# Order of the halves, and how q and k are loaded and transposed, in a sparse-attention and FFN kernel

## The chip, the core and the metric

The kernel runs on one core of a Trainium2 chip. Its engines work in parallel, each on its own queue of instructions in program order: TensorE (PE in the profile, PEld for its weight loads) multiplies and transposes, VectorE (DVE), ScalarE (ACT) and GpSimd (POOL) work element by element, and SyncE (SP) only issues DMAs. ACT and POOL can issue DMAs too. Engines wait for each other on semaphores. SBUF is the working memory with 128 partitions; PSUM holds what TensorE writes. The metric is the device time of one execution in microseconds (us).

## The reference

Four batches, 8 heads, 768 tokens, head dimension 64. Keys are cut into 24 chunks of 32 tokens. For each query an upper bound of its scores in each chunk is made from the chunk's smallest and largest keys; the six best chunks that are not in the future are kept, and softmax attention runs over these alone. The result, as 3072 rows of 512, goes through an FFN with a squared ReLU.

```python
k_min, k_max = min and max of k over each chunk
ub = np.sum(np.maximum(q[:, :, :, None, :] * k_min[:, :, None, :, :],
                       q[:, :, :, None, :] * k_max[:, :, None, :, :]), axis=-1)
ub = np.where(causal, ub, -1000000000.0)
top_chunks = np.argsort(ub, axis=-1)[..., -top_k:]
mask = sel & (pos[:, None] >= pos[None, :])
scores = np.where(mask, scale * q @ k.T, -1000000000.0)
attn = softmax(scores)
x = (attn @ v), heads side by side          # (3072, 512)
h = np.maximum(x @ w_in, 0.0)               # (3072, 2048)
out = h * h @ w_out                         # (3072, 512)
```

## The kernel before

**Tiles and slots.** A half is 384 tokens of one batch (`HB`, three blocks of 128). The work is cut into 32 slots `s`, each one pair of heads `p` of one half, four slots to a half and eight halves, in the order batch 0 first half, batch 0 second half, batch 1 first half, and so on. By causality a first half needs 6 pairs of blocks (query block, key block) a head, a second half 15; these I call light and heavy.

**One slot.** `step_P` gets queries and keys with the head dimension on the partitions, and relu(-q) and relu(q) of the queries. Chunk minima and maxima land in `kbds`. `step_U` multiplies these into the bounds `ub`, takes the sixth largest by MAX8 and writes which chunks fall out (`nsel`). `step_V` transposes that (`qt`) and copies it into the rows of `kqs` beside the queries, where fixed code rows (`codes`) stand beside the keys: a score of an unselected chunk so becomes hugely negative. `step_E` makes scores `ps` and ACT's exponentials `e` (POOL masks the diagonal), `step_F` multiplies with the values `vn` into `po`, and DVE divides into `x` (L386).

**Which way keys and queries are transposed.** The first two halves (`ON_PE = 2`) are transposed on TensorE, a 128x128 block at a time (`step_T`, L204): three for k and three for q in each slot. From PSUM, `step_T2` makes the relus on ACT (L212, L213), the chunk extrema on DVE (`extrema`, L181 and L182), and `place` copies keys (DVE) and queries (ACT) into `kqs` (L222). From the third half on, a DMA transpose issued by SP (`tr`, L250) writes `kqT`, two more DMAs place it in `kqs` (`place_dma`, L234), DVE makes the relus (`relus`, L245 and L246) and folds the chunks of a whole half in steps (`step_K`, L266, parts spread over a slot or two).

**Loads.** POOL issues them and converts fp32 to bf16 in the DMA. A load of k or q (`load_n`, L85) brings 128 tokens of all heads, so each contiguous run is one token of one head, 64 elements. Values come four heads at a time over all 768 tokens (`load_v`, L101). `w_in` and `w_out` come in two loads each. The first two pairs of the first half are loaded as fp32 by SP and ACT and cast on chip.

**The order of the work is written out by hand.** `later` maps a slot to what is issued at two points of it (`go`): loads, DMA transposes, code DMAs. The FFN of a half starts when its attention ends (`step_X` transposes `x`, on TensorE for the first, second and last half, by DMA otherwise); its pieces, 16 up products (L431, ReLU on ACT at L438, for half of the first half's on DVE at L436, square on DVE at L440) and 12 down pieces (L450), stand in `queue` and are taken by `f1` between the steps of later slots, by a `quota` for each slot. The up products share two PSUM buffers (`psF`), the down products one (`psY`), the rest of attention two (`psA`) and the scores three (`psS`).

Of the kernel before, what the change touches and what calls it, by code (L numbers as in the profile page):

```python
# [14 lines left out]
CH = 32  # L15
# [13 lines left out]
ON_PE = 2  # L29
# [5 lines left out]
def kernel(  # L35
# [40 lines left out]
    kn0 = epool.tile([128, HT, NP, 2 * D], BF16, tag="kn0", name="kn0")  # L76
# [6 lines left out]
    def load_n(n, b, j):  # L83
        t = nat[n, b, j] = work.tile([128, DM], BF16, tag=f"{n}n", bufs=7, name=f"{n}n")
        nc.gpsimd.dma_start(  # L85
            out=t.rearrange("p (h d) -> p h d", d=D),
            in_=(q if n == "q" else k)[b, :, 128 * j:128 * (j + 1)]
            .rearrange("h p d -> p h d"))

    def load_k0(j):  # L90
        nc.gpsimd.dma_start(
            out=kn0[:, j, 2:NP, :].rearrange("p a (h d) -> p (a h) d", h=2),
            in_=k[0, 4:H, 128 * j:128 * (j + 1)].rearrange("h p d -> p h d"))
# [10 lines left out]


    staged = {}
    for p, n in ((0, "k"), (0, "q"), (1, "k"), (1, "q")):
        x = epool.tile([128, HT, 2, D], F32, tag=f"st{n}{p}", name="stage")
        for hh in range(2):
            (nc.sync if n == "k" or p else nc.scalar).dma_start(  # L110
                out=x[:, :, hh, :],
                in_=(k if n == "k" else q)[0, 2 * p + hh, 0:HB]
                .rearrange("(j p) d -> p j d", p=128))
        staged[n, p] = x
# [6 lines left out]
    make_identity(nc, ident)  # L121
    for j in range(HT):
        load_k0(j)
        for h in range(2):
            load_q0(j, h)
    load_v(0, 0, 4)
# [46 lines left out]
    slots = [(b, half, p) for b in range(B) for half in range(2) for p in range(NP)]  # L173
# [3 lines left out]
    def extrema(kt, s):  # L177
        b, half, p = slots[s]
        km = work.tile([128, 2, 12], BF16, tag="km", name="km")
        kv = kt.rearrange("p (c j) -> p c j", j=CH)  # L180
        nc.vector.tensor_reduce(km[:, 0, :], kv, axis=AX.X, op=ALU.min)  # L181
        nc.vector.tensor_reduce(km[:, 1, :], kv, axis=AX.X, op=ALU.max)  # L182
# [3 lines left out]

    def step_cast(p):
        nc.vector.tensor_copy(kn0[:, :, p, :].rearrange("p j (h d) -> p j h d", h=2),
                              staged["k", p])
        nc.scalar.copy(qn0[:, :, p, 1:3, :], staged["q", p])  # L190

    def step_T(s, kp, qp):

        b, half, p = slots[s]
        t = st.setdefault(s, {})
        for n, (pool, tag) in enumerate((kp, qp)):
            x = t["kq"[n]] = pool.tile([128, HB], BF16, tag=tag, name="t" + "kq"[n])
            for j in range(HT):
                if s < NP:
                    src = (qn0[:, j, p, 1:3, :].rearrange("p h d -> p (h d)") if n  # L200
                           else kn0[:, j, p, :])
                else:
                    src = nat["kq"[n], b, HT * half + j][:, 128 * p:128 * (p + 1)]
                nc.tensor.matmul(x[:, 128 * j:128 * (j + 1)], lhsT=src, rhs=ident,  # L204
                                 is_transpose=True, start=True, stop=True)

    def step_T2(s):
# [4 lines left out]
        nc.scalar.activation(qr[:, 0, c:], t["q"][:, c:], ACT.Relu, scale=-1.0)  # L212
        nc.scalar.activation(qr[:, 1, c:], t["q"][:, c:], ACT.Relu)  # L213
# [5 lines left out]
    def place(s, n, copy):  # L219
        b, half, p = slots[s]  # L220
        for h in range(2):
            copy(kqs[b % 2][QROW[h]:QROW[h] + D, h, p, 2 * half + "kq".index(n), :],  # L222
                 st[s][n][D * h:D * h + D])
# [8 lines left out]
    def place_dma(hb):  # L232
        for h in range(2):
            nc.sync.dma_start(  # L234
                out=kqs[hb // 2 % 2][QROW[h]:QROW[h] + D, h, :,
                                     2 * (hb % 2):2 * (hb % 2) + 2, :],
                in_=half_T(hb)[D * h:D * h + D])

    def relus(s):
        hb, p = s // NP, s % NP  # L240
        qT = tT[hb][:, p, 1, :]
        c = 128 * (1 - hb % 2)
# [5 lines left out]
    def tr(hb, n, j):  # L248
        b, half = hb // 2, hb % 2
        nc.sync.dma_start_transpose(  # L250
            out=half_T(hb)[:, :, "kq".index(n), 128 * j:128 * (j + 1)],
            in_=nat.pop((n, b, HT * half + j)))

    def step_K(hb):

        b, half = hb // 2, hb % 2
# [24 lines left out]
    def step_P(s):  # L281
# [3 lines left out]
        step_T(s, *((F, Y) if s < NP + 2 else (Y, A)))  # L285
# [109 lines left out]
    def step_X(hb, pe):  # L395
# [21 lines left out]
        for c in ("u" * NFI) if hb == 0 else "ddudu" "duuduud" "uuduuduu" "uuuu":  # L417
# [10 lines left out]
    def ffn_up(hb, xT, f):  # L428
# [6 lines left out]
        if hb == 0 and f % 2:  # L435
            nc.vector.tensor_scalar_max(ht, ph[:, 0:HB], 0.0)  # L436
        else:
            nc.scalar.activation(ht, ph[:, 0:HB], ACT.Relu)  # L438
# [4 lines left out]
    def ffn_down(hb, py, t, c, act, tail):  # L443
# [9 lines left out]
        if c == 3:  # L453
# [5 lines left out]
            r0 = HB * hb + 128 * t  # L459
# [22 lines left out]
    def load_half(hb):  # L482
        b, half = hb // 2, hb % 2
        return [(load_n, n, b, HT * half + j) for n in "kq" for j in range(HT)]

    for i, x in enumerate(load_half(1)):
        at(i // 3 - 1, *x)
    at(1, load_v, 0, 4, 8)
    for g in range(2):
        at(1, load_w_in, 1024 * g, 1024 * g + 1024)  # L490
    for i, x in enumerate(load_half(2)):
        at(2 + i // 3, *x)
    at(0, codes, 0, 1, nc.sync.dma_start)
    at(1, clear)
    for half in range(2):
        at(2, codes, 1, half, nc.sync.dma_start)
# [159 lines left out]
```

## Time and profile before

| | us |
|---|---|
| median of three runs | 306.0 (303.69 to 306.05) |
| profiled execution, its own time | 306.22 |
| span of that execution in the profile | 304.5 |
| TensorE busy | 257.7 |
| ScalarE busy | 172.4 |
| VectorE busy | 168.4 |
| GpSimd busy | 92.6 |

The mean granted clock of TensorE was 0.966 of full speed. A row of the profile names line, engine and operation, the tile written and the tiles read, then how many, the busy time, the mean in ns, and the idle time of the engine before them with what ended it. Matmul ends are modelled, so the pace of a run of matmuls is read from start to start.

### The profile page before, as it was taken

The numbers are of one execution on the slowest core, as the hardware profiler recorded it, in microseconds if no ns is written. First come the engines' busy times: TensorE is split into PE (matmuls) and PEld (weight loads), VectorE is DVE, ScalarE is ACT, GpSimd is POOL, SyncE is SP. The second block draws the span as 40 slices with busy tenths as digits, with TensorE's granted clock in tenths as the row PEclk, the third lists the DMA queues.
The fourth block names the chain that finished last, engine by engine and source line by source line (L and its number), as shares of the span: only waits on it lengthen the run. The fifth ranks groups of instructions, "written<-read, shape, count | busy, mean of one in ns | idle before, by whom it ended". The sixth has DMA issues, their size and how long they took to land.

```text
span 304.5 us, 6200 instructions
## 1 busy us (share of the span) xinstructions
PE 257.7 (85%) x2232; PEld 156.6 (51%) x2260; DVE 168.4 (55%) x657; ACT 172.4 (57%) x370; POOL 92.6 (30%) x133
## 2 busy tenths in 40 slices
PE   1576798398939969998969979998979999999994
PEld 1355465155515636665526636665546566655541
DVE  6668597583266625854276626753497445433421
ACT  4559398245606646784536648783547667843410
POOL 8868322123932133443331223530112101100000
PEclk9997799899969999999989999999999999999999
DMA  9999999969999095899989198694661310101001
GB/s 159 174 132 174 196 166 196 156 102 109 119 156 139 35 153 102 96 175 120 141 131 128 22 155 108 115 171 68 133 138 38 86 37 0 37 31 40 34 36 69
DMA packets 114062, 33.30 MB, mean 109 GB/s; under 512 B 103280, under 2 KB 109936, under 8 KB 114032
## 3 DMA queue, kind: packets, MB, share of 16 engines
q0 software_dynamic: 74736, 13.24, 60.5%
q1 hardware_dynamic: 38496, 19.47, 31.4%
q8 instruction: 17, 0.28, 0.4%
q10 hardware_dynamic: 800, 0.20, 0.3%
q14 instruction: 13, 0.11, 0.1%
HBM read 27.26 MB, written 6.29 MB: 110 GB/s over the span
## 4 chain that ended last, share of the span: by engine, by line
PE 55%; DMA 21%; DVE 10%; issue 4%; ACT 3%; SPq 3%; POOL 2%; POOLq 0%; ACTq 0%
PE py L450 20%; PE ph L431 20%; DMA kqT<-kn 8%; PE ps L351 8%; DMA kn<-in_k_dram 6%; PE po L376 5%; DMA vn<-in_v_dram 4%; DMA xT<-x 3%; DVE km L266 3%; DVE h L440 2%; ACT e L356 2%; DVE x L386 1%; SPq L413 1%; SPq L250 1%; POOL qn L96 1%
## 5 line engine op out<-in xcount | busy, mean ns | idle before, releaser
L356 ACT ACTIVATE e<-ps 128x512 bf16<-128x512 f32 x192 | 96.8, 549 | 51.6 <-PE ps L351 51.5
L431 PE MATMUL ph<-xT,w_in 128*128 128x384 bf16 x512 | 104.7, 333 | 9.6 <-DVE ht L436 5.1
L450 PE MATMUL py<-w_out,h 128*128 128x512 bf16 x356 | 92.6, 383 | 3.6 <-ACT ob L456 2.1
L360 POOL TENSOR_SCALAR_AFFINE_SELECT e<-e 128x384 bf16<-128x384 bf16 x64 | 34.0, 532 | 168.2 <-ACT e L356 165.9
L438 ACT ACTIVATE ht<-ph 128x384 bf16<-128x384 f32 x120 | 59.5, 502 | 44.4 <-PE ph L431 43.9
L440 DVE TENSOR_TENSOR h<-ht 128x384 bf16<-128x384 bf16 x128 | 47.9, 375 | 61.3 <-ACT ht L438 60.7
L431 PEld LDWEIGHTS <-w_in 128*128 128x128 bf16 x512 | 47.7, 99 | 40.1 <-issue 14.5
L351 PE MATMUL ps<-kq 128*128 128x384 bf16 (+2 forms) x320 | 59.7, 291 | 3.4 <-DVE kq L327 2.1
L450 PEld LDWEIGHTS <-h 128*128 128x128 bf16 x384 | 35.6, 98 | 34.8 <-issue 3.7
L351 PEld LDWEIGHTS <-kq 128*128 128x128 bf16 x320 | 28.4, 102 | 23.9 <-issue 4.6
L376 PEld LDWEIGHTS <-e 128*128 128x128 bf16 x672 | 26.5, 100 | 6.2 <-issue 1.6
L376 PE MATMUL po<-vn,e 128*128 128x65 bf16 x672 | 27.8, 196 | 1.1 <-DMA vn<-in_v_dram 0.8
L305 DVE MAX8 m<-ub 128x8 f32<-128x24 f32 (+1 forms) x160 | 16.6, 171 | 11.7 <-PE ub L298 11.6
L85 POOL DMA_DIRECT2D kn<-in_k_dram x21 | 18.9, 906 | 0.3 <-issue 0.2
L85 POOL DMA_DIRECT2D qn<-in_q_dram x21 | 18.6, 892 | 0.1
L333 PE MATMUL qt<-ident,nsel 128*128 128x128 bf16 x72 | 9.0, 226 | 11.3 <-DVE nsel L306 11.2
L386 DVE TENSOR_TENSOR x<-po,r 128x384 bf16<-128x384 f32 x32 | 17.8, 558 | 1.1
L266 DVE TENSOR_TENSOR km<-kqT 128x768 bf16<-128x768 bf16 x12 | 6.7, 558 | 18.2 <-DMA kqT<-kn 11.8
L456 ACT COPY ob<-py 128x512 f32<-128x512 f32 x19 | 11.1, 585 | 9.6 <-PE py L450 9.5
L337 DVE COPY kq<-qt 64x384 bf16<-64x384 bf16 (+1 forms) x28 | 8.8, 315 | 13.1 <-PE qt L333 13.1
L333 PEld LDWEIGHTS <-nsel 128*128 128x128 bf16 x72 | 5.4, 99 | 18.2 <-DVE nsel L306 15.6
L266 DVE TENSOR_TENSOR km<-km 128x384 bf16<-128x384 bf16 (+3 forms) x48 | 13.2, 274 | 0.8
(59 smaller groups left out, 163.9 us busy)
## 6 DMA issues: line engine op xcount, KB each, us to landing
out_dram<-ob SPq DMA_DIRECT2D x24, 256.0 KB, 2.2
kq<-kqT SPq DMA_DIRECT2D x12, 384.0 KB, 5.5
vn<-in_v_dram POOLq DMA_DIRECT2D x8, 384.0 KB, 9.0
kn<-in_k_dram POOLq DMA_DIRECT2D x21, 128.0 KB, 5.0
qn<-in_q_dram POOLq DMA_DIRECT2D x21, 128.0 KB, 7.3
w_in<-in_moe_w_in_dram POOLq DMA_DIRECT2D x2, 1024.0 KB, 12.6
w_out<-in_moe_w_out_dram POOLq DMA_DIRECT2D x2, 1024.0 KB, 17.6
kq<-oneh SPq DMA_DIRECT2D x6, 192.0 KB, 7.4
```

Source lines behind the costliest of these rows:

```text
L85: nc.gpsimd.dma_start(out=t.rearrange("p (h d) -> p h d", d=D), in_=(q if n == "q" else k)[b, :, 128 * j:128 * (j + 1)] .rearrange("h p d ...
L266: nc.vector.tensor_tensor(y, x[:, :, :, 0:m], x[:, :, :, m:2 * m], op=op)
L305: nc.vector.max(out=m8[:, j, hh, :], in_=ub[:, j - j0, hh, :])
L351: nc.tensor.matmul(ps[:, at:at + 128 * m], lhsT=kqs[b % 2][:, hh, p, 2 * (j // HT), 128 * (j % HT):128 * (j % HT + 1)], rhs=qc(s, hh)[:, c ...
L356: nc.scalar.activation(e[:, 512 * n + lo:512 * n + hi], ps[:, lo:hi], ACT.Exp, scale=float(scale))
L360: nc.gpsimd.affine_select(out=d, in_=d, compare_op=ALU.is_ge, fill=0.0, base=0, channel_multiplier=-1, pattern=[[0, 3], [1, 128]])
L376: nc.tensor.matmul(po[:, hh, i, :], lhsT=t["e"][hh][:, c:c + 128], rhs=vn[b % 2][:, 2 * p + hh, j, :], start=(j == 0), stop=(j == iq))
L386: nc.vector.tensor_mul(x[:, :, 128 * p:128 * (p + 1)].rearrange("p j (h d) -> p h j d", h=2), po[:, :, :, 0:D], r.to_broadcast([128, 2, HT ...
L431: nc.tensor.matmul(ph[:, 0:HB], lhsT=w_in[:, ki, 128 * f:128 * (f + 1)], rhs=xT[:, ki, :], start=(ki == 0), stop=(ki == NKI - 1))
L438: nc.scalar.activation(ht, ph[:, 0:HB], ACT.Relu)
L440: nc.vector.tensor_mul(h, ht, ht)
L450: nc.tensor.matmul(py[t], lhsT=h2[hb, f][:, 128 * t:128 * (t + 1)], rhs=w_out[:, f, :], start=(f == 0), stop=(f == NFI - 1))
```

## The change

Four things change together. The halves come in the order (batch 0 first, batch 1 first, batch 0 second, batch 1 second), then batches two and three as before (`ORDER`); the second half in time is now a light one and the third a heavy one. Three halves instead of two are transposed on TensorE (`ON_PE = 3`). For these, except the queries of the first, a load puts 4 consecutive tokens of a head on one of 96 partitions (`load_packed`), and a head's 64 columns are transposed 96 tokens at a time (16 transposes a slot instead of 6). The transposed tokens so lie in four strides of 96, and `extrema`, the relus and `place` read them from PSUM in token order. The issue times of nearly all loads, the values' loads (a block of 128 tokens of all heads at a time for the first two batches), the code DMAs, the order of the FFN's pieces and the quotas move with it, and all ReLUs of the FFN go to ACT.

```diff
+ORDER = ((0, 0), (1, 0), (0, 1), (1, 1), (2, 0), (2, 1), (3, 0), (3, 1))
-ON_PE = 2
+ON_PE = 3
+TP = 4
+PP = HB // TP
...
+    def load_packed(n, g, h0=0):
         nc.gpsimd.dma_start(
+            out=packed(n, g)[:, h0:H],
+            in_=rows(n, *ORDER[g], h0, H).rearrange("h (p j) d -> p h (j d)", j=TP))
...
+    def load_vt(b, j):
+        nc.gpsimd.dma_start(
+            out=vn[b % 2][:, :, j, 0:D],
+            in_=v[b, :, 128 * j:128 * (j + 1)].rearrange("h p d -> p h d"))
...
-        kv = kt.rearrange("p (c j) -> p c j", j=CH)
-        nc.vector.tensor_reduce(km[:, 0, :], kv, axis=AX.X, op=ALU.min)
+        kv = kt.rearrange("r (j c e) -> r c j e", j=TP, c=12)
+        nc.vector.tensor_reduce(km[:, 0, :], kv, axis=AX.XY, op=ALU.min)
...
+    def in_order(x):
+        return x.rearrange("r (j p) -> r p j", j=TP)
...
+            for hh in range(2):
+                for j in range(TP):
+                    nc.tensor.matmul(
+                        x[D * hh:D * hh + D, PP * j:PP * j + PP],
+                        lhsT=packed(n, s // NP)[:, 2 * p + hh, D * j:D * j + D],
+                        rhs=ident[0:PP, 0:PP], is_transpose=True, start=True, stop=True)
...
+        for w in range(2):
+            o, i = qr[:, w, c:], t["q"][:, c:]
+            if s >= NP:
+                o, i = by_token(o), in_order(t["q"])[:, c // TP:, :]
+            nc.scalar.activation(o, i, ACT.Relu, scale=(-1.0, 1.0)[w])
...
-            copy(kqs[b % 2][QROW[h]:QROW[h] + D, h, p, 2 * half + "kq".index(n), :],
-                 st[s][n][D * h:D * h + D])
+            copy(by_token(kqs[b % 2][QROW[h]:QROW[h] + D, h, p, 2 * half + "kq".index(n), :]),
+                 in_order(st[s][n][D * h:D * h + D]))
...
-        step_T(s, *((F, Y) if s < NP + 2 else (Y, A)))
+        step_T(s, *((F, Y) if s < NP + 2 else (Y, A) if s < 2 * NP + 1 else (F, A)))
...
-        for c in ("u" * NFI) if hb == 0 else "ddudu" "duuduud" "uuduuduu" "uuuu":
+        for c in ("u" * NFI) if hb == 0 else "dddd" + "uud" * 4 + "u" * 8:
...
-        if hb == 0 and f % 2:
-            nc.vector.tensor_scalar_max(ht, ph[:, 0:HB], 0.0)
-        else:
-            nc.scalar.activation(ht, ph[:, 0:HB], ACT.Relu)
+        nc.scalar.activation(ht, ph[:, 0:HB], ACT.Relu)
...
+    for n in "kq":
+        at(-1, load_packed, n, 1)
     for g in range(2):
-        at(1, load_w_in, 1024 * g, 1024 * g + 1024)
+        at(0, load_w_in, 1024 * g, 1024 * g + 1024)
+    at(0, codes, 1, 0, nc.sync.dma_start)
     at(1, clear)
+    for j in range(HT):
+        at(1, load_vt, 1, j)
+    for n in "kq":
+        at(2, load_packed, n, 2)
+    at(3, codes, 0, 1, nc.sync.dma_start)
     for g in range(2):
-        at(3 + g, load_w_out, 8 * g, 8 * g + 8)
+        at(3, load_w_out, 8 * g, 8 * g + 8)
+    for j in range(HT):
+        at(5, load_vt, 0, HT + j)
+        at(6, load_n, "k", 3, j)
+        at(8, load_n, "q", 3, j)
+        at(9, load_vt, 1, HT + j)
+    at(7, codes, 1, 1, nc.sync.dma_start)
+    for g in range(4, 2 * B):
         for i in range(2 * HT):
+            at(4 * g - 6 + i // HT, load_n, "kq"[i // HT], g, i % HT)
...
-        quota = [(4, 5, 6, 5)[p] if hb == 1 else 9 if p == 0 and hb > 2 else
+        quota = [(4, 4, 4, 6)[p] if hb == 1 else 9 if p == 0 and hb > 2 else
                  7 if p == 3 else 6]
-        if hb < 2 * B - 1 and p == (2 if hb == 1 else 1):
+        if ON_PE - 1 <= hb < 2 * B - 1 and p == (2 if hb < ON_PE else 1):
             parts.extend(step_K(hb + 1))
```

123 lines of the change are left out of this document (55 added, 68 removed).

## The prediction

> **What bounds the kernel now.** I read the page first, then the windows, then the chain of waits, then the timeline around the gaps the chain showed. The page:
>
> ```profile
> span 304.5 us, 6200 instructions
> PE 257.7 (85%) x2232; PEld 156.6 (51%) x2260; DVE 168.4 (55%) x657; ACT 172.4 (57%) x370; POOL 92.6 (30%) x133
> PEclk9997799899969999999989999999999999999999
> DMA  9999999969999095899989198694661310101001
> ```
>
> TensorE (PE) is the bound on average, but not everywhere: the DMA row is full for about the first third, and the lowest clock digits lie in the same third. The windows (start:end, length, then busy us of PE, PEld, DVE, ACT and POOL, the clock, DMA share, GB/s) divide the run into the first half (four slots without FFN work), the second, the third, and all the rest, with three 10 us stretches of them:
>
> ```profile
> 0.00:33.50 33.50, 16.93 (x173) 12.70 (x174) 23.70 (x97) 20.09 (x46) 26.57 (x40) 0.95 1.83 165
> 33.50:73.00 39.50, 31.27 (x317) 20.20 (x320) 27.37 (x96) 23.27 (x48) 10.42 (x14) 0.91 1.38 156
> 73.00:105.40 32.40, 26.59 (x210) 15.28 (x212) 17.88 (x77) 16.19 (x35) 12.90 (x18) 0.89 1.12 113
> 105.40:304.50 199.10, 182.91 (x1539) 108.42 (x1558) 99.42 (x389) 112.89 (x241) 42.67 (x62) 0.99 0.66 90
> ...
> 40.00:50.00 10.00, 9.38 (x107) 6.46 (x105) 9.56 (x30) 9.32 (x21) 1.55 (x3) 1.00 1.41 181
> 50.00:60.00 10.00, 4.86 (x55) 2.82 (x52) 5.17 (x19) 4.39 (x9) 2.44 (x3) 0.92 1.60 169
> 80.00:90.00 10.00, 4.49 (x38) 2.63 (x36) 3.86 (x18) 2.91 (x8) 4.32 (x6) 0.78 2.01 164
> ```
>
> After 105.4 us PE is busy 92% of the time (182.91 of 199.10) and nothing there is edited but load times. What can be won lies before: 50 to 60 and 80 to 90 have PE at half. The chain says what these wait for:
>
> ```profile
> 25.61 12.98 DMA kn<-in_k_dram
> 41.30 15.19 DMA kqT<-kn
> 70.33 5.21 DMA kn<-in_k_dram
> 76.81 5.36 DMA kqT<-kn
> ```
>
> A load of keys, then a DMA transpose of them, once for the third half and once for the fourth. The timeline shows how that reaches PE:
>
> ```profile
> 56.52 0.56 DVE L266 TENSOR_TENSOR km<-kqT 128x768 bf16<-128x768 bf16 x1 [4.63 <-DMA kqT<-kn]
> 58.56 1.44 PE L431 MATMUL ph<-xT,w_in 128*128 128x384 bf16 x4 [4.52 <-DVE ht L436]
> 61.45 1.62 PE L431 MATMUL ph<-xT,w_in 128*128 128x384 bf16 x8
> 85.94 0.56 DVE L266 TENSOR_TENSOR km<-kqT 128x768 bf16<-128x768 bf16 x1 [6.24 <-issue]
> 89.03 0.40 PE L333 MATMUL qt<-ident,nsel 128*128 128x128 bf16 x2 [5.45 <-DVE nsel L306]
> 91.56 1.27 PE L431 MATMUL ph<-xT,w_in 128*128 128x384 bf16 x4
> 93.05 0.81 PE L431 MATMUL ph<-xT,w_in 128*128 128x384 bf16 x4
> ```
>
> The fold of the keys (L266) stands at the head of VectorE's (DVE's) queue and waits for the transposes; FFN and selection work stands behind it, and PE runs dry for 4.52 and 5.45 us. Afterwards the granted clock is at half for a while: four matmuls take 1.44 and 1.27 us against 0.81.
>
> **What goes.** The third half no longer goes through a DMA transpose, so the first wait has no cause left. The fourth half (still by DMA) is loaded from slot 6 and 8 and transposed in slots 8 and 9, two slots ahead of its fold in slot 10, where before the fold of the third came in slot 6 behind loads queued with w_in. And the loads ahead of it shrink:
>
> ```profile
> DMA packets 114062, 33.30 MB, mean 109 GB/s; under 512 B 103280, under 2 KB 109936, under 8 KB 114032
> w_out<-in_moe_w_out_dram POOLq DMA_DIRECT2D x2, 1024.0 KB, 17.6
> ```
>
> Nine packets in ten are under 512 B. A half of k or of q is 3 x 128 tokens x 8 heads = 3072 runs of one token; four tokens to a partition makes 96 x 8 = 768. The k and q of halves two and three and most keys of the first go that way, six DMA transposes and the two placing DMAs of the third vanish, and the values of batch 0's second half move to slot 5. I price these loads at what waits for them, not by bytes.
>
> Stall 1: 4.52 idle, and half speed from 58.56 to about 61.4, which loses half of 2.9, 1.4. Stall 2: 5.45, and half speed from 89.03 to about 92.8, 1.9. Together **-13.3 us**. If a load is late all the same, the fourth half's fold is what waits next (a rival below).
>
> In the first half two transposes waited for loads:
>
> ```profile
> 13.91 0.29 PE L204 MATMUL tk<-ident,kn 128*128 128x128 bf16 x1 [1.36 <-DMA kn<-in_k_dram]
> 15.28 0.29 PE L204 MATMUL tq<-ident,qn 128*128 128x128 bf16 x1 [0.86 <-DMA qn<-in_q_dram]
> ```
>
> One packed load for keys and all of q before v, with four of six code DMAs gone from SP's early queue, should land both before they are needed: 1.36 + 0.86 = 2.2; less a little for the added transposes, **-2.0**.
>
> **What is added on PE.** A pair needs 2 heads x 4 = 8 transposes for k and 8 for q, against 3 and 3, and against none in the third half. First half: +5 x 4 = 20; second: +10 x 4 = 40; third: 16 x 4 = 64; 124 in all. The 20 of the first half and the 20 of slots 4 and 5 (made in slots 2 and 3) fall where PE is busy 16.93 of 33.5 us and cost nothing; without that cover they cost 2.8. The other 84 lie on the path. No 96x64 transpose is in the trace. The nearest are these, three 128x128 transposes in 0.17 us from start to start, 57 ns each, and the weight loads:
>
> ```profile
> 40.16 0.33 PE L204 MATMUL tk<-ident,kn 128*128 128x128 bf16 x3
> 40.33 0.33 PE L204 MATMUL tq<-ident,qn 128*128 128x128 bf16 x3
> 40.50 0.81 PE L431 MATMUL ph<-xT,w_in 128*128 128x384 bf16 x4
> ...
> L204 PE MATMUL tk<-ident,kn 128*128 128x128 bf16 x24 | 3.6, 263 | 7.7 <-DVE kn L188 6.4 <-DMA kn<-in_k_dram 1.4
> ```
>
> By columns it would be 57 x 96/128 = 43 ns; as thinly as the 24 rows ran, 3.6/24 = 150 ns. I take 70, nearer the dense row because these too come in runs of eight: 84 x 70 = **+5.9** (3.6 to 12.6).
>
> The Trainium skill ("TensorE: Matmul & The Clock Gate", section "Weight-path perf modes") says the fast weight load needs a full 128-column weight, and these have 64; by its section "LDWEIGHTS" (columns/1.2) each takes 53 ns to load. Added to 43 ns of matmul unhidden, an estimate of 96 ns, the term would be 8.1; no run so far shows a 64-column load.
>
> **What is added on DVE and ScalarE (ACT).** These rows:
>
> ```profile
> L438 ACT ACTIVATE ht<-ph 128x384 bf16<-128x384 f32 x120 | 59.5, 502 | 44.4 <-PE ph L431 43.9 <-DVE nsel L306 0.4
> L181 DVE TENSOR_REDUCE km<-tk 128x12 bf16<-128x384 bf16 x8 | 4.4, 554 | 1.3 <-PE tk L204 1.2
> L213 ACT ACTIVATE qr<-tq 128x384 bf16<-128x384 bf16 x4 | 2.1, 516 | 0.0
> L222 ACT COPY kq<-tq 64x384 bf16<-64x384 bf16 x8 | 3.8, 473 | 0.1
> L222 DVE COPY kq<-tk 64x384 bf16<-64x384 bf16 x8 | 2.8, 355 | 0.1
> L436 DVE TENSOR_SCALAR ht<-ph 128x384 bf16<-128x384 f32 x8 | 4.4, 555 | 0.7 <-PE ph L431 0.6
> ```
>
> ACT gets two relus (0.516) and two query placements (0.473) in each slot of the third half, 1.98 x 4 = 7.9, and the eight relus of the FFN that DVE did, 8 x 0.502 = 4.0: 11.9 us. It was busy 23.27 + 16.19 of the 71.9 us of halves two and three, so it holds 51.4 of about 64. DVE gets two reductions and two key placements a slot of the third half, 2 x 0.554 + 2 x 0.355 = 1.8, times 4 is 7.3; it loses the 4.4 of L436 and the fold. So no engine is full. But 40 to 50 us shows PE, DVE and ACT over 93% busy at once with PE losing 0.6 us in 10. Bounds: 0 (hidden) to 11.9 (nothing hidden); I take PE's loss in that row over some 25 us of heavy slots, **+1.5**. The order also adds a wait: keys of slots 9 to 11 go into one of the two buffers of the FFN's first product (psF) until DVE has reduced and placed them, about 1.8 us each; on PE the next FFN product, and all behind it, can stand for that buffer. 0 to 5.4; I take half of the 0.50 (L438) in which ACT empties one, 0.25, thrice: **+0.8**.
>
> The strided copy has a row to either side: 355 ns for a copy, 554 ns for a reduction of the same 384 columns. At the second, place costs 0.4 us more a slot on DVE, which has room.
>
> The Trainium skill ("VectorE: DVE Perf Modes", section "Mode 2×_1P") asks step 1 for two 16-bit elements a cycle, which reading every 96th column breaks; it would put the copy at the second row. The 355 against 554 here agrees with such a mode for the unstrided copy.
>
> Orders that cost nothing: heavy and light halves only change places; by the quotas (20+25 pieces of FFN before, 18+25 after) one up and one down product are done later instead of earlier, at the same price on PE. POOL issues 2 DMAs for a half instead of 6, with its masks queued behind fewer. Values in three loads instead of one half-height load are 3072 packets either way. SP loses eight DMAs around the third half. Loads for halves four on are 2 slots ahead of their transposes; PE's 92% there I leave.
>
> **Sum.** -13.3 - 2.0 + 5.9 + 1.5 + 0.8 = -7.1. The profiled execution took 306.2 us for a span of 304.5 and stands 0.2 over the median of 306.0, so **299 us**.
>
> **Rivals.** (a) *More is won.* Transposes at 43 ns (3.6), no engine waits, and a less loaded DMA when the attention output is transposed at 105 us:
>
> ```profile
> 107.98 5.40 DMA xT<-x
> ```
>
> The fourth half's q and the fifth half's k are off the queues by then, and 5.40 could fall to about 3, -2.4: -13.3 - 2.2 + 3.6 - 2.4 = -14.3, 292. Against it: three engines at 93% do not run without waits. (b) *The stall only moves.* w_out (17.6 us to land, its row above) is now issued in slot 3 with the packed loads just ahead, and the fourth half's keys queue behind it; if they come late, the fold in slot 10 holds DVE as at 85.94, and stall 2 (7.4) stays: +0.3, 306. For it: half the chain there is DMA today. Against: four slots lie between load and fold. This is also the case in which packing does nothing, since bytes and not packets set the loads. (c) *Slower: reading PSUM in token order.* Every relu, reduction and placement of halves two and three now reads with a stride of 96. If that runs at half rate, ACT pays 1.98 and DVE 1.8 more a slot; in eight slots, with all three engines near full, the larger is on the path: 15.8, so -7.1 + 15.8 = +8.7, 315. It decides from about 0.9 us a slot, a strided operation 1.45 times as long. For it: no strided read of PSUM is in the trace, and DVE and ACT stood at 9.56 and 9.32 of 10. Against: ACT's time does not differ between 4-byte and 2-byte inputs (502, 516), so it seems to go by elements.
>
> **Numbers.** Forecast (294 to 303) 0.51; more (a, under 294) 0.13; moved stall (b, 303 to 309) 0.16; slower (c, over 309) 0.20. The range 290 to 311 leaves out the best of (a) and most of (c), together just under 0.2, and takes in the transposes' 12.6 (306) and an ACT term of 11.9 (309.5) by themselves. A measurement of this kernel can tell about 1%, 3 us, from no change. Faster: 0.51 + 0.13 = 0.64; within 1%: 0.16; slower: 0.20.
>
> **What would show it.** Right: no wait of DVE for kqT over 1 us before 105 us, the two waits at 13.9 and 15.3 gone, the third half over some 8 us before 105.4; PE busy some 6 to 9 us more in total; 96x64 transposes about 70 ns apart. (a) shows PE over 96% in halves two and three; (b) a wait for kqT or w_out near slot 10; (c) a relu or reduction well over 0.55 us and PE idle behind ACT or DVE. I am wrong if the waits go and the gain does not come: then the added work, not the loads, set these halves.

## The result, and the profile after

The changed kernel takes 294.45 us (median of 4 runs, 292.3 to 296.74), beside 306.02 us (303.69 to 306.85) for the kernel before on the same chip: a ratio of 0.961, 95% interval 0.952 to 0.970. It is 11.6 us faster where 7.1 were forecast. The profiled execution took 295.2 us, 1.8 more than its span. The page of it:

```profile
span 293.4 us, 6470 instructions
PE 260.4 (89%) x2384; PEld 159.8 (54%) x2384; DVE 172.0 (59%) x648; ACT 180.9 (62%) x393; POOL 87.4 (30%) x131
PEclk9999999999999999999999999999999999999999
DMA  8999999908999665999679966997451300010001
DMA packets 98671, 31.74 MB, mean 108 GB/s; under 512 B 84560, under 2 KB 94544, under 8 KB 98640
```

The clock row has no dip left after about 39 us, and TensorE is busy 2.7 us more in a span 11.1 us shorter. Before 39 us the row and the clock column say full speed where the matmuls ran at half of it; the part on the first half, below, shows this. One profile below, that of the unpacked loads, is of an execution over 1% slower (301.97 us) than its kernel's other ones, so only its waits are used, not its lengths. Where the 11.1 us went is read from windows that end with a half's attention, at the start of the last division into `x` (L386 before, L423 after). First the kernel before: the first, the second and the third half, then all the rest. The columns are the stretch, its length, the busy time of PE, PEld, DVE, ACT and POOL, the clock, the DMA share and GB/s.

```profile
0.00:32.90 32.90, 16.91 (x172) 12.68 (x172) 23.10 (x96) 20.09 (x46) 26.36 (x39) 0.95 1.84 164
32.90:72.00 39.10, 30.83 (x311) 19.87 (x313) 27.00 (x95) 23.27 (x48) 10.51 (x14) 0.91 1.40 160
72.00:104.80 32.80, 26.44 (x210) 15.28 (x213) 18.32 (x79) 16.19 (x35) 13.02 (x19) 0.90 1.13 113
104.80:304.50 199.70, 183.51 (x1543) 108.77 (x1562) 99.95 (x390) 112.89 (x241) 42.67 (x62) 0.99 0.65 90
```

The same four stretches of the changed kernel, where the light half now comes second and the heavy one third:

```profile
0.00:35.10 35.10, 20.07 (x207) 14.12 (x207) 23.12 (x94) 19.40 (x45) 21.55 (x35) 1.00 1.52 179
35.10:64.70 29.60, 24.25 (x253) 15.09 (x253) 23.01 (x76) 21.13 (x48) 9.27 (x14) 1.00 1.05 119
64.70:101.00 36.30, 32.86 (x357) 21.15 (x358) 24.28 (x90) 28.09 (x60) 14.38 (x20) 1.00 1.03 110
101.00:293.40 192.40, 183.21 (x1569) 109.39 (x1567) 101.56 (x391) 112.29 (x240) 42.23 (x62) 1.00 0.64 93
```

| stretch | before | after | difference | forecast |
|---|---|---|---|---|
| first half | 32.9 | 35.1 | +2.2 | -2.0 |
| halves two and three | 71.9 | 65.9 | -6.0 | -5.1 (-13.3 + 5.9 + 1.5 + 0.8) |
| the rest | 199.7 | 192.4 | -7.3 | 0 |

So the forecast was right where most of its working lay, had the wrong sign in the first half, and left out the largest single gain: the rest, where only the times at which loads are issued and the order of the FFN's pieces are edited. PE does the same work there (183.2 and 183.5 us busy) with 9.2 us idle in place of 16.2. The profile of the second measurement of the changed kernel, named below, has 33.8, 65.5 and 193.1 us for the three stretches: the last two hold, while the first varies by more than a microsecond.

### The profile page after: what moved, and what is told of

It is laid out like the page before. It is cut to its first block, busy times and chain, and to the rows that moved or that the text cites. A ratio compares the mean times of both kernels' runs of the same rounds, so it can differ in the third digit from the quotient of the medians.

```text
span 293.4 us, 6470 instructions
## 1 busy us (share of the span) xinstructions
PE 260.4 (89%) x2384; PEld 159.8 (54%) x2384; DVE 172.0 (59%) x648; ACT 180.9 (62%) x393; POOL 87.4 (30%) x131
## 4 chain that ended last, share of the span: by engine, by line
PE 62%; DVE 10%; DMA 9%; ACT 9%; SPq 4%; issue 3%; POOL 1%; ACTq 0%; DVEq 0%; POOLq 0%
PE py L484 22%; PE ph L468 22%; PE ps L388 8%; DMA qn<-in_q_dram 7%; PE po L413 7%; ACT e L393 4%; ACT ht L472 2%; DMA kqT<-kn 2%; SPq L450 2%; SPq L287 2%; DVE x L423 2%; DVE h L474 1%; DVE kq L260 1%; PE ub L335 1%; PE qt L370 1%
## 5 line engine op out<-in xcount | busy, mean ns | idle before, releaser
L468 PE MATMUL ph<-xT,w_in 128*128 128x384 bf16 x512 | 102.0, 329 | 3.7 <-ACT ht L472 3.1
L397 POOL TENSOR_SCALAR_AFFINE_SELECT e<-e 128x384 bf16<-128x384 bf16 x64 | 33.4, 521 | 162.9 <-ACT e L393 162.9
L472 ACT ACTIVATE ht<-ph 128x384 bf16<-128x384 f32 x128 | 63.4, 502 | 28.5 <-PE ph L468 26.6
L474 DVE TENSOR_TENSOR h<-ht 128x384 bf16<-128x384 bf16 x128 | 47.2, 373 | 57.3 <-ACT ht L472 56.8
L468 PEld LDWEIGHTS <-w_in 128*128 128x128 bf16 x512 | 47.5, 98 | 33.3 <-issue 6.6
L423 DVE TENSOR_TENSOR x<-po,r 128x384 bf16<-128x384 f32 x32 | 17.9, 558 | 1.1
L105 POOL DMA_DIRECT2D kn<-in_k_dram x15 | 13.3, 886 | 0.4 <-issue 0.3
L105 POOL DMA_DIRECT2D qn<-in_q_dram x15 | 13.2, 885 | 0.1
L492 DVE COPY ob<-py 128x512 f32<-128x512 f32 x6 | 4.2, 692 | 12.4 <-PE py L484 12.4
L303 DVE TENSOR_TENSOR km<-km 128x384 bf16<-128x384 bf16 (+3 forms) x40 | 10.6, 265 | 0.7
L121 POOL DMA_DIRECT2D vn<-in_v_dram x12 | 10.6, 888 | 1.2 <-DMA kn<-in_k_dram 1.1
```

Of the source, the lines that this page charges most:

```text
L105: nc.gpsimd.dma_start(out=nat_of(n, g)[:, DM * j:DM * j + DM].rearrange("p (h d) -> p h d", d=D), in_=rows(n, *ORDER[g], 0, H)[:, 128 * j: ...
L397: nc.gpsimd.affine_select(out=d, in_=d, compare_op=ALU.is_ge, fill=0.0, base=0, channel_multiplier=-1, pattern=[[0, 3], [1, 128]])
L423: nc.vector.tensor_mul(x[:, :, 128 * p:128 * (p + 1)].rearrange("p j (h d) -> p h j d", h=2), po[:, :, :, 0:D], r.to_broadcast([128, 2, HT ...
L468: nc.tensor.matmul(ph[:, 0:HB], lhsT=w_in[:, ki, 128 * f:128 * (f + 1)], rhs=xT[:, ki, :], start=(ki == 0), stop=(ki == NKI - 1))
L474: nc.vector.tensor_mul(h, ht, ht)
```

## The experiments

Four questions: what removed the stalls, what the added work costs, why the first half got longer, and where the rest won 7 us. Ratios are to the kernel before, run beside each kernel on the same chip; 0.01 is 3.1 us. The chips differ a little (the kernel before took 308.0, 305.9 and 305.7 us as the median of the three sets), so ratios are compared, not times. A second measurement of the changed kernel came out as the first, 294.44 us and 0.961 (0.955 to 0.967):

> The changed kernel itself, as the measure for the three beside it on this chip: a ratio of 0.955 to 0.966 to the kernel before.

**The stalls.** The third half goes back to DMA transposes, with everything else as changed.

```diff
-ON_PE = 3
+ON_PE = 2
-        at(2, load_packed, n, 2)
+        for j in range(HT):
+            at(2, load_n, n, 2, j)
-        if ON_PE - 1 <= hb < 2 * B - 1 and p == (2 if hb < ON_PE else 1):
+        if ON_PE - 1 <= hb < 2 * B - 1 and p == (2 if hb < 3 else 1):
```

> The changed kernel (294.5 us) with the third half again loaded 128 tokens at a time and transposed by DMA; all else stays. Theory of the prediction (the wait of the keys' fold is what the change removed): the fold in slot 6 waits again on DVE for kqT, some 3 to 5 us, PE runs dry behind it, and against that 64 transposes of some 45 ns (2.9 us) and ScalarE's 7.9 us of relus and placements are saved: 297 to 301 us. Rival (with the loads packed ahead of it the wait would be small anyhow, and the added work on three engines is what costs): at most 1 us of wait and 290 to 293 us.

It took 297.37 us, 0.966 (0.960 to 0.972). The stall did not come back in its old place; another came earlier. The timeline of PE has it:

```profile
34.52 0.98 PE L413 MATMUL po<-vn,e 128*128 128x65 bf16 x12 [5.18 <-POOL e L397]
```

PE waits for POOL to mask the exponentials, and POOL stood on a load. With everything behind it 5 us later, the fold of the third half's keys (at 51.99 us here) waits for nothing. The same shows more plainly in the next kernel, which keeps all three halves on TensorE but loads halves two and three 128 tokens at a time, three 128x128 transposes each, as the kernel before does, and reads them unstrided:

```diff
-        at(-1, load_packed, n, 1)
+        for j in range(HT):
+            at(-1, load_n, n, 1, j)
...
-        at(2, load_packed, n, 2)
+        for j in range(HT):
+            at(2, load_n, n, 2, j)
...
+            if s >= NP:
+                for j in range(HT):
+                    nc.tensor.matmul(
+                        x[:, 128 * j:128 * (j + 1)],
+                        lhsT=nat[n, s // NP][:, DM * j + 128 * p:DM * j + 128 * (p + 1)],
+                        rhs=ident, is_transpose=True, start=True, stop=True)
+                continue
```

> The changed kernel (294.5 us) with halves two and three loaded 128 tokens at a time and transposed as 128x128 blocks, 6 a slot instead of 16, and read from PSUM in order. Theory (the loads are what packing is for): k and q of the second half land 3 us or more later than at 22 and 25 us, PE waits for them in slot 2, and the total is 296 to 299 us. Rival (packing costs more on PE and DVE than it brings in the loads): key placement back at 355 ns, PE busy 3 to 4 us less, 290 to 293 us.

297.73 us, 0.968 (0.963 to 0.974). Its timeline, POOL's loads and masks and then PE:

```profile
20.93 1.51 POOL L519 DMA_DIRECT2D w_in<-in_moe_w_in_dram  x2
31.31 0.88 POOL L105 DMA_DIRECT2D qn<-in_q_dram  x1 [1.22 <-DMA w_in<-in_moe_w_in_dram]
36.27 1.78 POOL L105 DMA_DIRECT2D qn<-in_q_dram  x2 [4.08 <-DMA w_in<-in_moe_w_in_dram]
38.05 1.01 POOL L409 TENSOR_SCALAR_AFFINE_SELECT e<-e 128x384 bf16<-128x384 bf16 x2
38.65 0.98 PE L425 MATMUL po<-vn,e 128*128 128x65 bf16 x12 [6.37 <-POOL e L409]
```

The two `w_in` loads are the 17th and 18th that POOL issues in this kernel, the two that wait the 25th and 26th: a load on POOL stands until the eighth before it has landed, whatever the two have to do with each other, and the masks behind it stand too. The kernel before has the same: its 26th and 27th loads stand 1.41 and 3.23 us for its 18th and 19th. Whether the chip or the program sets the eight, no run shows. So I moved the queries of the third half one slot later, past the masks, in both kernels (`at(2 if n == "k" else 3, load_n, n, 2, j)`). On TensorE and unpacked:

> The unpacked kernel with the three query loads of the third half issued one slot later (slot 3), behind the masks that stood in POOL's queue behind them. Theory (what packing brings is 8 fewer DMA issues on POOL; with 6 loads to a half the eighth DMA after w_in waits for w_in to land, as L105 waiting 4.1 and L524 before it show, and masks and PE wait behind it): the 6.4 us gap of PE at the third step of po goes to under 1.5, first FFN product near 35 to 36 us, and the ratio to the kernel before is 0.950 to 0.962. Rival (bytes and packets: k and q of halves two and three land too late when unpacked): the gap moves to a wait for kn or qn and the ratio stays at 0.965 or more.

292.29 us, 0.956 (0.950 to 0.963), no slower than the change itself. The load still stands 3.85 us on POOL, but no mask waits behind it while PE needs one. And with the third half by DMA transpose:

> The kernel with the third half by DMA transpose, its three query loads issued one slot later, behind the masks. Theory (the wait of the keys' fold had already gone by the order and the earlier loads, and what was left of that kernel's loss was POOL standing on a load): the 5.2 us gap of PE goes to under 1.5 and the ratio is 0.945 to 0.957, faster than the change, since 64 transposes on PE and 7.9 us of ScalarE are saved. Rival (the DMA transposes of the queries then come too late and DVE waits for kqT in slots 6 to 8): 2 us or more of wait there, ratio 0.96 to 0.975.

299.76 us, 0.975 (0.966 to 0.984): the theory written beforehand was wrong, and the wait of its rival came. With POOL's trouble out of the way, the old stall is back at nearly its old place, in the timeline of DVE and PE:

```profile
54.60 0.56 DVE L303 TENSOR_TENSOR km<-kqT 128x768 bf16<-128x768 bf16 x1 [6.64 <-DMA kqT<-kn]
...
58.07 0.39 PE L370 MATMUL qt<-ident,nsel 128*128 128x128 bf16 x2 [8.73 <-DVE nsel L343]
```

Between these two kernels lie 0.0185, some 5.7 us (2 to 9 by the two intervals), for transposing the third half on TensorE rather than by DMA. The second half is loaded packed in the one with the DMA transpose and unpacked in the other, so they do not differ in one thing alone; but the wait in the trace is that of the prediction. The trace is of one of four executions (295.69 to 300.99 us); whether all have the stall is not on record. The second stall, that of the fourth half, is in no kernel here that loads this half earlier, but that edit was not tried alone. Packing by itself wins nothing that can be told from the noise: unpacked loads, placed so that no mask stands behind a waiting load, are as fast, though the keys of a half then need three loads and 3072 runs in place of one load and 768. What packing does save is loads in POOL's queue.

The order of the halves, put back with its value loads and code DMAs:

```diff
-ORDER = ((0, 0), (1, 0), (0, 1), (1, 1), (2, 0), (2, 1), (3, 0), (3, 1))
+ORDER = ((0, 0), (0, 1), (1, 0), (1, 1), (2, 0), (2, 1), (3, 0), (3, 1))
-    at(0, codes, 1, 0, nc.sync.dma_start)
+    at(0, codes, 0, 1, nc.sync.dma_start)
-        at(1, load_vt, 1, j)
+        at(1, load_vt, 0, HT + j)
-    at(3, codes, 0, 1, nc.sync.dma_start)
+    at(3, codes, 1, 0, nc.sync.dma_start)
-        at(5, load_vt, 0, HT + j)
+        at(5, load_vt, 1, j)
```

> The changed kernel (294.5 us) with the halves in the old order (batch 0 second half in second place, batch 1 first half in third), values and code rows loaded to match. Theory (the order is not what won; heavy and light halves only change places): 293.5 to 296 us, the second half longer and the third shorter by about 7 us. Rival (the light half in second place is what gives the loads their time): 298 us or more, with waits for loads in the second half.

294.98 us, 0.962 (0.955 to 0.970), where the change has 0.961. The order of the halves is worth nothing that can be told from the noise, which here is some 3 us; the heavy second half takes 4.7 us more than the light one did, the light third half 3.4 less than the heavy one.

**The added work.** The ReLUs of the first half's FFN shared with DVE again:

```diff
-        nc.scalar.activation(ht, ph[:, 0:HB], ACT.Relu)
+        if hb == 0 and f % 2:
+            nc.vector.tensor_scalar_max(ht, ph[:, 0:HB], 0.0)
+        else:
+            nc.scalar.activation(ht, ph[:, 0:HB], ACT.Relu)
```

> The changed kernel with every second ReLU of the first half's FFN back on DVE, as before the change. Theory (ScalarE's added work in halves two and three is hidden, so where these eight run is immaterial; the prediction gave all of ScalarE's added 11.9 us a price of 1.5): within 1 us of the changed kernel beside it, the second half 29 to 30.5 us. Rival (ScalarE sets the second half): 1.5 to 4 us faster, the second half under 28.

296.35 us, 0.966 (0.961 to 0.971): if anything slower, against 0.961 for the change in the same set; the second half takes 30.6 us against 29.6 and 29.2 in the two profiles of the change. So the eight ReLUs, 4.0 of ACT's added 11.9 us, do not set the second half. The other 7.9 us, in the third half, were not taken off ACT alone; with the third half by DMA transpose, the first kernel above, which takes these and the 64 transposes away, that half takes 33.6 us in place of 36.3. By these profiles the added work costs the third half some 2.7 us; the second half is 2.2 longer there (31.8 against 29.6), with waits of 2.06 and 2.19 us behind the selection and the fold. And the FFN's pieces in their old order:

```diff
-        for c in ("u" * NFI) if hb == 0 else "dddd" + "uud" * 4 + "u" * 8:
+        for c in ("u" * NFI) if hb == 0 else "ddudu" "duuduud" "uuduuduu" "uuuu":
```

> The changed kernel with the FFN's pieces in the old order. Theory (of the 7 us won after the third half, some 4 are the load times and the rest is carried by other things, the order of pieces among them): 0 to 2 us slower, ratio 0.961 to 0.968. Rival (the order of the pieces is immaterial): ratio within 0.958 to 0.963 and the halves four to six as long as in the changed kernel (33.5, 27.6, 32.9).

297.11 us, 0.971 (0.966 to 0.976). By the ratios the new order is worth some 3 us, though the ends of the two intervals overlap by a little. By the profile it is less: 0.7 to 2.0 us of the difference lie in the first half (35.8 us against 35.1 and 33.8), which has no FFN work. One gap of its timeline is 1.91 us, which is 0.88 in the changed kernel; the rest is spread thin and I could not name it:

```profile
82.83 0.81 PE L468 MATMUL ph<-xT,w_in 128*128 128x384 bf16 x4 [1.91 <-ACT ht L472]
```

**The first half.** In the changed kernel the timeline shows what the code DMAs and the first transposes do:

```profile
2.76 6.27 SPq L159 DMA_DIRECT2D kq<-oneh  x6
14.46 0.27 PE L230 MATMUL tq<-ident,qn 128*128 128x128 bf16 x1 [1.37 <-DMA qn<-in_q_dram]
20.12 0.54 PE L413 MATMUL po<-vn,e 128*128 128x65 bf16 x7 [0.76 <-DMA vn<-in_v_dram]
25.13 0.54 PE L237 MATMUL tq<-ident,qn 96*64 96x96 bf16 x8 [0.95 <-DMA qn<-in_q_dram]
```

All six code DMAs leave between 2.76 and 9.0 us, although the code writes four of them in slots 3 and 7: SP had nothing ahead of them to wait for. Slots order the instructions of an engine, not its time. So I had POOL issue those four, whose queue is busy until then:

```diff
-    at(3, codes, 0, 1, nc.sync.dma_start)
+    at(3, codes, 0, 1, nc.gpsimd.dma_start)
...
-    at(7, codes, 1, 1, nc.sync.dma_start)
+    at(7, codes, 1, 1, nc.gpsimd.dma_start)
```

> The changed kernel with the four code DMAs of slots 3 and 7 issued from POOL instead of SP. Theory (the prediction's -2.0 us in the first half failed because SP, with nothing ahead in its queue, issued all six code DMAs at 2.8 to 8.9 us, so that they ran beside the loads of q and v, whatever slot they were written in): SP issues two, q's last load lands 2 us earlier than 14.3 us and the last load of v 2 us earlier than 20.1, the waits of tq (1.37) and po (1.1) go, the first half ends 2 to 3 us earlier, ratio 0.952 to 0.958. Rival (SBUF to SBUF copies cost the loads nothing): landing times within 0.7 us and ratio 0.96 to 0.965.

291.81 us, 0.954 (0.949 to 0.959). Its timeline and its first window:

```profile
2.77 1.36 SPq L159 DMA_DIRECT2D kq<-oneh  x2
12.88 0.50 PE L230 MATMUL tq<-ident,qn 128*128 128x128 bf16 x3
27.01 1.26 POOL L159 DMA_DIRECT2D kq<-oneh  x2
```

```profile
0.00:31.20 31.20, 17.75 (x207) 12.61 (x207) 23.09 (x93) 19.18 (x45) 22.24 (x37) 0.91 1.49 174
```

The three transposes at 12.88 wait for nothing now, no other matmul of the first half waits for a load, and it ends at 31.2 in place of 35.1, with the same 207 matmuls: late loads, not the number of transposes, are most of the difference, since the four waits for loads in the changed kernel come to 3.45 us. How strong this is: it is one profile of each. In five other profiles with the loads packed and all six code DMAs early, the first half ends between 33.3 and 35.8 us, and in two of the kernel before (the second with new load times for later halves) at 32.9 and 33.4. For the whole run, the intervals of this 0.954 and of the change's 0.961 overlap.

The pace of TensorE differs too. Five products of scores, first in the changed kernel, then in the one with the code copies late:

```profile
22.00 1.23 PE L388 MATMUL ps<-kq 128*128 128x384 bf16 x5 [0.70 <-DVE kq L364]
19.94 0.70 PE L388 MATMUL ps<-kq 128*128 128x384 bf16 x5 [0.86 <-DVE kq L364]
```

In the kernel before five of them take 1.23 us at 26.32, where the clock column has 0.50, and 0.71 at 21.78, where it has 1.00. So the changed kernel ran at half speed at 22.00, although the column has 1.00 there; its FFN products keep that pace until about 39 us (six take 2.08 us at 37.38, eight 1.66 at 39.66). The kernel before has the same mismatch up to about 20 us.

The end at 31.2 is 1.7 below the kernel before, near the 2.0 forecast. But the kernel before had five waits for loads in its first half, 3.4 us in all, and all of their kind are gone; the other 1.7 us are added work or slower pace, which no run separates. The pages' rows of DMA issues say how far copies within the chip's memory delay a load beside them; first the changed kernel (KB each, median us from issue to landing):

```profile
w_in<-in_moe_w_in_dram POOLq DMA_DIRECT2D x2, 1024.0 KB, 17.0
```

and with the code copies late:

```profile
w_in<-in_moe_w_in_dram POOLq DMA_DIRECT2D x2, 1024.0 KB, 12.0
```

In the five other profiles with packed loads and early code copies this is 14.8 to 17.5 us.

**The rest.** The loads of halves six to eight issued as before (two a slot from eight slots before the half, in place of three a slot from six before), all else as changed:

```diff
-            at(4 * g - 6 + i // HT, load_n, "kq"[i // HT], g, i % HT)
+            at(4 * g - 6 + i // HT if g == 4 else 4 * g - 8 + i // 2, load_n,
+               "kq"[i // HT], g, i % HT)
```

> The changed kernel (294.5 us) with the loads of halves six to eight in time issued over three slots, as before the change (two each in the first, second and third slot of a half, where the DMA transposes of the attention output and of the keys are issued too). Theory (the 7 us that were won after the third half, which the prediction did not have, come from these loads no longer running beside those transposes): 297 to 300 us, and waits for xT or kqT of 1 to 3 us return at the starts of halves five to seven. Rival (they come from the order of the FFN's pieces, or from what carries over from the third half): 294 to 295.5 us.

298.63 us, 0.972 (0.967 to 0.977): some 3.3 us of the gain are lost (1 to 6 by the intervals of this kernel and of the changed one's second measurement). And the other way round, the kernel before with only these load times:

```diff
-            at(4 * hb - 8 + i // 2, *x)
+            at(4 * hb - 8 + i // 2 if hb == 4 else 4 * hb - 6 + i // 3, *x)
```

> The kernel before, with only the loads of halves six to eight issued two slots later and over two slots, as the change does. Theory (what the change won after the third half came from these load times, and needs nothing else of it): 3 to 5 us faster than before, ratio 0.984 to 0.990, the fifth and sixth half in time 2 to 4 us shorter together and the waits for xT and kqT there under 1.5 us. Rival (it needs the new order of the FFN's pieces too): ratio 0.995 to 1.005.

299.41 us, 0.977 (0.971 to 0.983). One line gives 7.1 us (5.3 to 8.9), and both its first stalls are still there. The windows of halves four and five say where: the kernel before,

```profile
104.80:172.30 67.50, 60.84 (x534) 36.61 (x540) 37.59 (x156) 39.90 (x86) 21.72 (x30) 0.97 1.05 118
```

the kernel before with the new load times,

```profile
104.30:166.70 62.40, 59.89 (x542) 35.87 (x540) 37.34 (x157) 39.88 (x86) 21.65 (x30) 1.00 1.07 128
```

the changed kernel,

```profile
101.00:162.10 61.10, 59.83 (x545) 36.69 (x544) 37.76 (x157) 39.93 (x86) 21.62 (x30) 1.00 0.97 127
```

and the changed kernel with the old load times:

```profile
100.90:166.70 65.80, 61.27 (x538) 37.37 (x544) 37.99 (x157) 39.94 (x86) 21.64 (x30) 0.97 1.00 121
```

67.5 and 65.8 us with the old times, 62.4 and 61.1 with the new, for the same work, and the DMA engines as busy in all four: when the loads run matters here, not how many there are. The timeline of the kernel before shows the mechanism:

```profile
105.40 4.95 SPq L413 DMA_TRANSPOSE xT<-x  x3
107.23 1.78 POOL L85 DMA_DIRECT2D kn<-in_k_dram  x2
113.51 0.81 PE L431 MATMUL ph<-xT,w_in 128*128 128x384 bf16 x4 [2.41 <-DMA xT<-x]
...
145.91 3.83 SPq L250 DMA_TRANSPOSE kqT<-kn  x3
147.18 0.89 POOL L85 DMA_DIRECT2D kn<-in_k_dram  x1
153.52 0.56 DVE L266 TENSOR_TENSOR km<-kqT 128x768 bf16<-128x768 bf16 x1 [4.17 <-DMA kqT<-kn]
156.61 0.28 PE L333 MATMUL qt<-ident,nsel 128*128 128x128 bf16 x2 [2.81 <-DVE nsel L306]
```

Twice a load starts beside DMA transposes, the transposes come late, and PE runs dry, for 2.41 and 2.81 us. The second of these is the stall of the third and fourth halves once more, in miniature: the fold at the head of DVE's queue (4.17 us), the selection behind it, PE behind that, and a lower clock. In the changed kernel `xT` is transposed at 101.63 and the next load comes at 120.35:

```profile
101.63 3.86 SPq L450 DMA_TRANSPOSE xT<-x  x3
120.35 1.42 POOL L116 DMA_DIRECT2D vn<-in_v_dram  x1 [0.22 <-issue]
```

PE has no gap over 0.6 us between 104 and 163 us there. With the old load times a load is issued at 103.74, and the chain of waits has `xT` again:

```profile
104.09 6.28 DMA xT<-x
```

In the profiles, the load times are enough for the whole gain of the rest: it takes 199.7 us in the kernel before, 192.6 in the kernel before with the new load times, which keeps the old order of the FFN's pieces, and 192.4 in the changed kernel. Taking the load times back costs less, 3.3 us by the ratios and 3.9 to 4.6 in the profiles' rest (197.0 against 193.1 and 192.4). The fifth half's loads are new in that kernel and old in the other; they were not tried alone, and how the gain divides among the halves' loads stays open.

**The best version.** Late code copies (slots 4 and 7) and unpacked loads with late queries, together:

```diff
-    at(3, codes, 0, 1, nc.sync.dma_start)
+    at(4, codes, 0, 1, nc.gpsimd.dma_start)
-    at(7, codes, 1, 1, nc.sync.dma_start)
+    at(7, codes, 1, 1, nc.gpsimd.dma_start)
-        at(2, load_packed, n, 2)
+        for j in range(HT):
+            at(2 if n == "k" else 3, load_n, n, 2, j)
```

> The two edits that won together: codes of later slots issued from POOL (slots 4 and 7), and halves two and three unpacked with the third half's queries one slot later. Theory (both act on the start of the run, but on different things: the first on what runs beside the first loads, the second on TensorE's 10 extra transposes a slot and on DVE's strided placement): first half over at 30 to 32 us, ratio 0.945 to 0.955, at or a little below 0.954. Rival (unpacked loads take the room that the codes leave): 0.956 or more.

290.88 us (290.67 to 291.33), 0.950 (0.945 to 0.954), where the change in the same set took 293.45 to 294.88. It keeps the transposes on TensorE, the FFN's order and the load times, and drops the packing for halves two and three. It is clearly faster than the change. Against either edit alone (0.954 and 0.956) the intervals overlap, and its first half ends at 32.2 us, a little over what was expected.

## Why the prediction came out as it did

The forecast of a gain stands, and its chief mechanism is shown. Its size is right only in part: two terms failed in opposite directions, and the larger was one that I had priced at nothing.

**The two stalls (-13.3): right.** Both gaps of PE are gone, and so is the half speed after them: from 42 us to the end of the third half every run of four up products takes 0.81 or 0.82 us. DVE's wait for the transposed keys is gone before 105 us and has shrunk to this over the whole run (total, times, longest), where the kernel before had 11.8 us in three waits besides the 6.24 at 85.94:

```profile
DVE km L303 <- DMA kqT<-kn: 4.8, 4, 2.2
```

The row at 85.94 names no releaser (`<-issue`), so that it stood for the keys is inferred: the third of their transposes was issued at 80.7, and the six of this half took up to 6.0 us to land. Rival (b), a stall that only moves, so fell for the packed version. It was nearer than I had thought: with four loads more in POOL's queue, a stall of 5 to 6 us stands at 34 to 38 us, behind POOL's masks and not behind the fold.

**The transposes (+5.9): mis-sized.** In the timeline of the changed kernel:

```profile
48.12 0.37 PE L237 MATMUL tk<-ident,kn 96*64 96x96 bf16 x8
48.31 0.36 PE L237 MATMUL tq<-ident,qn 96*64 96x96 bf16 x8
48.60 0.82 PE L468 MATMUL ph<-xT,w_in 128*128 128x384 bf16 x4
```

Sixteen take 0.48 us from the first to the next matmul, 30 ns each in place of 70; the 84 on the path come to 2.5 us. The lower bound by columns (43 ns) was too high as well: the pace of the 128x128 rows does not carry over by the columns streamed; why not, no run here shows. The estimate of 96 ns worked out from the Trainium skill ("TensorE: Matmul & The Clock Gate", section "LDWEIGHTS") is refuted for this form: eight weight loads of 64 columns took 0.24 us, 30 ns each, less than the 53 ns that section would give one:

```profile
48.11 0.24 PEld L237 LDWEIGHTS <-kn 96*64 96x64 bf16 x8 [0.16 <-issue]
```

**Waits of the engines (+1.5 + 0.8): too small by about 2.** PE's idle time in halves two and three fell from 14.6 to 8.8 us, by 5.8, while the two gaps alone had 9.97: so some 4.1 us of new idle time came, mostly in gaps of 0.9 to 1.2 us behind `x`, `nsel`, `kbd` and `ht`. With the transposes that is 2.5 + 4.1 = 6.6 where I had 8.2, and -13.3 + 6.6 = -6.7 against the -6.0 measured. (One bound of the prediction is off by a little: an ACT term of 11.9 by itself gives 309.3, not 309.5.)

**Strided reads: rival (c) fell.** The groups of the changed kernel:

```profile
L260 DVE COPY kq<-tk 64x384 bf16<-64x384 bf16 x16 | 8.9, 555 | 0.3
L205 DVE TENSOR_REDUCE km<-tk 128x12 bf16<-128x384 bf16 x12 | 6.7, 556 | 1.5 <-PE tk L237 1.3
L251 ACT ACTIVATE qr<-tq 128x384 bf16<-128x384 bf16 x8 | 3.6, 508 | 0.2
L260 ACT COPY kq<-tq 64x384 bf16<-64x384 bf16 x16 | 7.6, 474 | 0.2
```

Only DVE's copy got longer, 355 to 555 ns; the reduction (554), ACT's relu (516) and ACT's copy (473) did not change. That is the second of the two rows between which I had left it. It agrees with the Trainium skill's page "VectorE: DVE Perf Modes", section "Mode 2×_1P", which asks for step one to make two results a cycle.

**The first half (-2.0): failed.** The step that failed is "four of six code DMAs gone from SP's early queue". They were not gone, as the row at 2.76 us shows. The keys came in time, and the first wait went with them. The wait for queries grew from 0.86 to 1.37 us, and three that I had not counted grew as well: those for values from 0.78 to 1.13 in all, that for the second half's queries from 0.36 to 0.95. All waits for loads together stayed the same, 3.36 us before and 3.45 after. With the copies late in fact, the half came out 1.7 shorter than before, so "cost nothing" for the 40 transposes made there is not shown either.

**Loads for halves four on (0): failed.** "PE's 92% there I leave" is the step. (Its "nothing there is edited but load times" also overlooked the order of the FFN's pieces, which the load times turned out not to need.) 8% of 199 us is 16 us of idle time, more than the whole forecast, and 5.2 us of it stood in two waits of the kind I had just worked out for the earlier halves. Rival (a) named one of them (`xT`, -2.4) and gave it to a different cause, queues emptied by earlier loads; the second, at 156.61 us, I did not look for.

**The signs named in advance.** No wait of DVE for `kqT` before 105 us and no wait at 13.9: held. The wait at 15.3 stayed, at 14.46. The third half was over 3.8 us earlier and not 8, PE was busy 2.7 us more and not 6 to 9, and the transposes came 30 ns apart and not 70. That the total still lies inside the range is in part luck: the first half missed by 4.2 us one way, the rest by 7.3 the other.

## What to carry to other kernels

When a stall's mechanism is found, look for it through the whole run, and in the stretch with a good average too: here PE ran dry four times behind a late DMA transpose, and one line about load times, which shrinks the two smaller gaps to 0.88 and 0.52 us, won 7 us by itself. A slot in hand-written order places an instruction behind others on its engine and nothing more; on an engine with an empty queue it starts at once, and what is to be late must be issued from a queue that is late. Before more loads go on a queue that also computes, count which load each will stand behind.

## What was not expected of the hardware

- In these programs a load issued by POOL stands until the eighth load before it on that queue has landed (4.08 us behind `w_in`), and POOL's own computation stands behind it.
- Transposes of 64 columns on 96 partitions ran at 24 to 36 ns each at 48 us, their weight loads included, where the 128x128 ones of before took 57.
- The profile's clock read 1.00 at the start of the run, to about 39 us in the changed kernel and 20 us in the kernel before, while matmuls took as long as at 0.50 (five score products 1.23 us, later 0.70).
- A DMA transpose of 128 tokens with a load beside it took 5.40 and 6.28 us in the chains (the two `xT` rows); where no load had been issued for some 9 us, the chain of the changed kernel has 2.49, and where none had been for some 16 us, that of the kernel before with the new load times has 3.86 (`xT` at 107.48):

```profile
142.29 2.49 DMA kqT<-kn
```
